# Long convolutions by a folded radix-8 DFT in an SSM and MLP kernel, forward and backward

## The chip, the cores and the metric

The kernel runs on one core of a Trainium2 chip. The metric is the device time of one execution in microseconds (us); lower is better. TensorE (PE) multiplies matrices, VectorE (DVE), ScalarE (ACT) and GpSimd (POOL) work on tiles of 128 partitions in SBUF, and the transfers (DMAs) of this program are issued by SyncE (SP) and, in the kernel before, by POOL too.

## The reference

A sequence of 2048 tokens with 512 channels runs twice through a layer normalisation, a gated long convolution and an MLP, with the same weights both times; the outputs are the result and the gradients of all inputs but B_x.

```python
def _A_ref(q, k, v, shift_k, ssm_k, ssm_D):
    for t in range(ks):                                  # ks = 4
        k_shift = k_shift + k_pad[:, t:t + S, :] * shift_k[:, ks - 1 - t][None, None, :]
    kv = k_shift * v
    L = 2 * S
    ...
    y_f = kv_f * kf_f[None, :, :, :]                     # rfft of length L of kv and of ssm_k, zero-padded
    y = irfft2(y_f, s=(1, L), ...).astype(jnp.bfloat16)[:, 0, :S, :]
    y = y + kv * ssm_D[None, None, :]
    return q * y

def _B_ref(x, w1, b1, w2, b2):
    h = _gelu(jnp.einsum("bsd,df->bsf", x, w1) + b1)     # F = 1376
    return jnp.einsum("bsf,fd->bsd", h, w2) + b2

x = A_q
x = x + _A_ref(_layernorm(x), A_k, A_v, A_shift_k, A_ssm_k, A_ssm_D)
x = x + _B_ref(_layernorm(x), B_w1, B_b1, B_w2, B_b2)
x = x + _A_ref(_layernorm(x), ...)
x = x + _B_ref(_layernorm(x), ...)
```

The convolution y depends on k, v and ssm_k alone, so it is computed once, and its result gates both layers. Backward, the gradient gy of y goes through the same convolution with a conjugated spectrum, which gives gkv (and from it the gradients of v, k and shift_k) and gh (of ssm_k).

## The kernel before, in words

The program has five parts, one after the other: the convolution forward (phase_conv_forward), the weights (load_weights), the MLP lanes forward and backward (phase_mlp: four slices of 512 tokens that run interleaved through both layers), the weight gradients (weight_grads), and the convolution backward (phase_conv_backward). A framework's scheduler sets the order of the instructions on each engine; an engine then takes its instructions strictly in that order, and SP issues its DMAs in that order too.

The long convolution is a real DFT of length 4096 written as dense matmuls. fwd_transform folds the 16 token tiles with their mirror images, tile a with tile 15-a, where the mirror is a matmul with an anti-identity into rev_ps and the sums P and differences M are made on DVE (L167, L168). Then it multiplies with cosine and sine tables for 8 blocks of even and 8 of odd frequencies: 8 matmuls into fwd_psc (L182) and 8 into fwd_pss (L185) for each of 16 pairs, 256 matmuls of 128x128 by 512 in all. It runs for h (ssm_k), for kv, and backward for gy. inv_transform does the same the other way in 264 matmuls (inv_A, L198 to L207); it runs for y, and backward for gkv and gh. The tables Fblk and Iblk have 8 MB each in bf16. gen_block_pair makes them: integer arguments on DVE and ACT (L132 to L137), sines on ACT (L138, L139). They are stored to DRAM (Fmat, Imat) and loaded again where they are used.

Around the transforms stand spec_products (six DVE instructions on 128x512 for each of 16 pieces of a spectrum, L228 to L240, the other operand streamed as sst from Hspec_d or KVspec_d), the shift convolution (four shifted loads kj of k for each tile, multiplied on DVE with Wbc, the shift weights broadcast to all partitions, L361 to L373), and backward process_gk, which shifts gks with matmuls (sh_ps), multiplies and adds on DVE (gk_tmp, gk_acc, L983 to L987), and gathers the shift weights' gradient with products on POOL (gw_prod, L994) and sums in f32 on DVE (gwacc, L995). WT_d (L303) is the shift weights transposed element by element in DRAM.

load_weights loads w1 and w2 and their transposes w1T and w2T from DRAM with DMA transposes; since 1376 is 10 x 128 + 96, the last 96 rows of w1T come as plain DMAs of 96x128 single elements (L543). The lanes read the tokens in natural order (x_sl, L827).

Of the kernel before, what the change touches and what calls it, by code (L numbers as in the profile page):

```python
# [11 lines left out]
ACT = mybir.ActivationFunctionType  # L12
# [36 lines left out]


def build_consts(nc, tc, const_pool, dims: Dims):
    c = Consts()
    S, L = dims.S, dims.L
    NJ = dims.NJ
    c.ident = const_pool.tile([P, P], BF16, name="ident")
    tmpf = const_pool.tile([P, P], F32, name="tmpf")
    nc.gpsimd.memset(tmpf, 0.0)
    nc.gpsimd.affine_select(out=tmpf, in_=tmpf, compare_op=ALU.not_equal, fill=1.0, base=0,
                            pattern=[[-1, P]], channel_multiplier=1)
    nc.vector.tensor_copy(out=c.ident, in_=tmpf)  # L60
    c.anti = const_pool.tile([P, P], BF16, name="anti")
    tmpf2 = const_pool.tile([P, P], F32, name="tmpf2")
    nc.gpsimd.memset(tmpf2, 0.0)
    nc.gpsimd.affine_select(out=tmpf2, in_=tmpf2, compare_op=ALU.not_equal, fill=1.0, base=-(P - 1),
                            pattern=[[1, P]], channel_multiplier=1)
    nc.vector.tensor_copy(out=c.anti, in_=tmpf2)
    alt_i = const_pool.tile([P, 4], I32, name="alt_i")
    nc.gpsimd.iota(alt_i[:, 0:1], pattern=[[0, 1]], base=0, channel_multiplier=1)
    altf = const_pool.tile([P, 4], F32, name="altf")
    nc.vector.tensor_copy(out=altf[:, 0:1], in_=alt_i[:, 0:1])  # L70
    nc.vector.tensor_single_scalar(out=alt_i[:, 1:2], in_=alt_i[:, 0:1], scalar=1, op=ALU.bitwise_and)
    nc.vector.tensor_copy(out=altf[:, 1:2], in_=alt_i[:, 1:2])
    nc.vector.tensor_scalar(out=altf[:, 2:3], in0=altf[:, 1:2], scalar1=-2.0, scalar2=1.0,
                            op0=ALU.mult, op1=ALU.add)
    c.altcol = const_pool.tile([P, 1], BF16, name="altcol")
    nc.vector.tensor_copy(out=c.altcol, in_=altf[:, 2:3])
    c.onescol = const_pool.tile([P, 1], BF16, name="onescol")
    nc.vector.memset(c.onescol, 1.0)
    c.onescol_f = const_pool.tile([P, 1], F32, name="onescol_f")
    nc.vector.memset(c.onescol_f, 1.0)  # L80
    hs_i = const_pool.tile([1, P], I32, name="hs_i")
    nc.gpsimd.iota(hs_i, pattern=[[1, P]], base=0, channel_multiplier=0)
    hs_f = const_pool.tile([1, P], F32, name="hs_f")
    nc.vector.tensor_single_scalar(out=hs_i, in_=hs_i, scalar=1, op=ALU.bitwise_and)
    nc.vector.tensor_copy(out=hs_f, in_=hs_i)
    nc.vector.tensor_scalar(out=hs_f, in0=hs_f, scalar1=-1.0, scalar2=0.5, op0=ALU.mult, op1=ALU.add)
    c.halfsign = const_pool.tile([1, P], BF16, name="halfsign")
    nc.vector.tensor_copy(out=c.halfsign, in_=hs_f)
    c.eps = const_pool.tile([P, 1], F32, name="eps")
    nc.vector.memset(c.eps, EPS_LN)  # L90
    c.SIN_EPS = 1e-6
    c.pibias = const_pool.tile([P, 1], F32, name="pibias")
    nc.vector.memset(c.pibias, math.pi * (1.0 - c.SIN_EPS))
    HT = dims.HT
    pv_i = const_pool.tile([P, 3 * HT], I32, name="pv_i")
    nc.gpsimd.iota(pv_i[:, 0:HT], pattern=[[2 * P, HT]], base=1, channel_multiplier=2)
    nc.gpsimd.iota(pv_i[:, HT:2 * HT], pattern=[[2 * P, HT]], base=0, channel_multiplier=2)
    nc.gpsimd.iota(pv_i[:, 2 * HT:3 * HT], pattern=[[2 * P, HT]], base=1, channel_multiplier=2)
    c.pv = const_pool.tile([P, 3 * HT], F32, name="pv")
    nc.vector.tensor_copy(out=c.pv, in_=pv_i)  # L100
    c.pvF = c.pv[:, 0:HT]
    c.pvIe = c.pv[:, HT:2 * HT]
    c.pvIo = c.pv[:, 2 * HT:3 * HT]
    ph_i = const_pool.tile([P, 2 * HT], I32, name="ph_i")
    nc.vector.tensor_single_scalar(out=ph_i, in_=pv_i[:, HT:3 * HT], scalar=L // 2, op=ALU.add)
    c.twc = const_pool.tile([P, 2 * HT], F32, name="twc")
    c.tws = const_pool.tile([P, 2 * HT], F32, name="tws")
    sin_scale = -(math.pi / L) * (1.0 - c.SIN_EPS)
    nc.scalar.activation(out=c.tws, in_=pv_i[:, HT:3 * HT], func=ACT.Sin, scale=sin_scale, bias=c.pibias)
    nc.scalar.activation(out=c.twc, in_=ph_i, func=ACT.Sin, scale=sin_scale, bias=c.pibias)  # L110
    c.ntwc = const_pool.tile([P, 2 * HT], F32, name="ntwc")
    nc.vector.tensor_single_scalar(out=c.ntwc, in_=c.twc, scalar=-1.0, op=ALU.mult)
    c.sin_scale = sin_scale
    return c


def build_row_tables(nc, pool, consts, dims):
    NJ = dims.NJ
    consts.row_e = pool.tile([P, NJ], F32, name="row_e")
    consts.row_o = pool.tile([P, NJ], F32, name="row_o")  # L120
    ri = pool.tile([P, NJ], I32, name="gen_ri")
    nc.gpsimd.iota(ri, pattern=[[2, NJ]], base=0, channel_multiplier=0)
    nc.vector.tensor_copy(out=consts.row_e, in_=ri)
    nc.gpsimd.iota(ri, pattern=[[2, NJ]], base=1, channel_multiplier=0)
    nc.vector.tensor_copy(out=consts.row_o, in_=ri)


def gen_block_pair(nc, tc, work_pool, consts: Consts, dims: Dims, row_tab, pv_col, out_cos, out_sin):
    NJ = dims.NJ
    L = dims.L  # L130
    u = work_pool.tile([P, NJ], I32, name="gen_u", tag="gen_u")
    nc.vector.tensor_scalar(out=u, in0=row_tab, scalar1=pv_col, scalar2=None, op0=ALU.mult)  # L132
    rs = work_pool.tile([P, NJ], I32, name="gen_rs", tag="gen_rs")
# [16 lines left out]
def gen_inverse_blocks(nc, tc, work_pool, consts, dims, dest_fn):  # L150
    for b in range(dims.HT):
# [3 lines left out]
                       dest_fn(Q_ICO, b), dest_fn(Q_ISO, b))  # L155


def fwd_transform(nc, tc, dims, consts, psum_pool, pm_pool, in_tiles, blocks, evac_pair, evac_nyq):
    D, HT, NT = dims.D, dims.HT, dims.NT
    Pt = []  # L160
    Mt = []
# [985 lines left out]
```

## Time and profile before

| | |
|---|---|
| median of 3 runs | 1572.46 us (1571.51 to 1572.75) |
| the profiled execution | 1560.17 us, its span 1558.4 us, mean granted TensorE clock 0.817 |
| busy | PE 989.9 us, DVE 920.9, ACT 503.9, POOL 259.5 |
| DMA | 213.44 MB in 329431 packets |

All rows of the prediction come from the one profiled execution. Its page lists busy time, the chain of work that ended last, and groups of instructions by line. In a windows row stand the stretch in us, its length, then for each engine its busy time and number of instructions, then the granted TensorE clock, the DMA share (the summed packet time against 16 DMA engines; it passes 1 where packets overlap) and GB/s. In a chain row stand start, length and what the path waited for. In a group's row stand line, engine, operation, output and inputs, shape, count, busy us, mean ns of one, and the idle time before it.

### The profile page before, as it was taken

To read this page: it belongs to the slowest core of one execution; us is meant where nothing else is said; L and a number is where in the kernel's file an instruction comes from. 1 tells how busy PE (TensorE), PEld (TensorE's weight loads), DVE (VectorE), ACT (ScalarE), POOL (GpSimd) and SP (SyncE) were. 2 spreads that over 40 slices of the span, in tenths; PEclk is the share of its full clock that TensorE was granted. 3 is DMA by queue.
4 is the path that set the end of the run, shared out by engine and by line. 5 is a ranking of instruction groups with operands and counts; after the bars stand their busy time and mean duration, and the time that the engine had idled before them with its cause. 6 is when DMAs were issued, how large, how long until landed. Compare 5 with 4: busy or idle time off the path is not lost.

```text
span 1558.4 us, 12837 instructions
## 1 busy us (share of the span) xinstructions
PE 989.9 (64%) x4028; PEld 403.3 (26%) x4109; DVE 920.9 (59%) x1840; ACT 503.9 (32%) x632; POOL 259.5 (17%) x369
## 2 busy tenths in 40 slices
PE   3557492095016688685998875999586276731097
PEld 2113141042002233232443332444132022200043
DVE  8669950721058999873788880000411699897921
ACT  7623471010007988892022230000022022221421
POOL 0036320020013111100001110000000055562000
PEclk9879696597557889997999987999688688865599
DMA  5557537407994464557785579898613421211201
GB/s 54 209 190 236 180 134 286 132 0 18 91 106 137 136 177 133 181 172 205 218 229 152 166 176 217 175 195 171 234 43 135 175 65 58 67 58 38 73 1 55
DMA packets 329431, 213.44 MB, mean 137 GB/s; under 512 B 213584, under 2 KB 322061, under 8 KB 328722
## 3 DMA queue, kind: packets, MB, share of 16 engines
q1 hardware_dynamic: 321474, 168.56, 46.3%
q0 software_dynamic: 7888, 44.05, 7.4%
q8 instruction: 32, 0.52, 0.1%
q14 instruction: 37, 0.30, 0.1%
HBM read 91.27 MB, written 85.67 MB: 114 GB/s over the span
## 4 chain that ended last, share of the span: by engine, by line
DVE 31%; PE 30%; DMA 15%; SPq 9%; issue 6%; ACT 5%; POOL 3%; another core or an unknown queue 1%; DVEq 0%; POOLq 0%; ACTq 0%
PE dw_ps L784 9%; PE fwd_psc L182 4%; PE fwd_pss L185 4%; DVE gwacc L995 3%; DVE gk_tmp L986 3%; DMA kj<-in_A_k_dram 2%; PE inv_A L198 2%; DMA KVspec_d<-KVspec 2%; SPq L541 2%; PE inv_A L200 2%; SPq L306 2%; PE gh_ps L694 2%; DMA sst<-Hspec_d 2%; PE inv_A L204 2%; PE inv_A L206 2%
## 5 line engine op out<-in xcount | busy, mean ns | idle before, releaser
L675 PE MATMUL o_ps<-w_sb,h_sl 128*128 128x512 bf16 x347 | 97.2, 422 | 32.6 <-DVE h_sl L644 32.1
L897 DVE TENSOR_TENSOR gd_prod<-gy_bf,kv_t 128x512 bf16<-128x512 bf16 x16 | 6.4, 424 | 172.8 <-PE gd_ps L898 166.1
L662 PE MATMUL z_ps<-nT_sl,w_sb 128*128 128x512 bf16 x342 | 83.1, 394 | 20.7 <-DMA nT_sl<-n_sl 14.4
L694 PE MATMUL gh_ps<-gT_sl,w2T_sb 128*128 128x512 bf16 x343 | 82.8, 387 | 20.5 <-DMA gT_sl<-G 19.5
L784 PEld LDWEIGHTS <-dw_tm 128*128 128x128 bf16 x704 | 69.1, 98 | 102.6 <-DMA dw_tm<-h_d 18.0
L784 PE MATMUL dw_ps<-G,dw_tm 128*128 128x512 bf16 x345 | 77.9, 386 | 17.9 <-DMA dw_tm<-h_d 17.5
L705 PE MATMUL gn_ps<-w1T_sb,gz_sl 128*128 128x512 bf16 x346 | 82.1, 383 | 0.2
L696 DVE SCALAR_TENSOR_TENSOR gz_sl<-gh_ps,gpb 128x512 bf16<-128x512 f32 x88 | 58.3, 688 | 30.5 <-PE gh_ps L694 26.6
L784 PE MATMUL dw_ps<-dw_n,dw_tm 128*128 128x512 bf16 x345 | 75.8, 379 | 0.4
L672 PE MATMUL o_ps<-x_sl,ident 128*128 128x512 bf16 x32 | 13.5, 421 | 89.7 <-DVE x_sl L621 87.4
L750 ACT ACTIVATE nb_sl<-nb_sl,ab_ab 128x512 bf16<-128x512 bf16 x32 | 23.4, 802 | 145.1 <-DVE bb_junk L708 125.6
L994 POOL TENSOR_TENSOR gw_prod<-sh_bf,k_t 128x512 bf16<-128x512 bf16 x48 | 58.9, 1229 | 43.5 <-DVE gwacc L995 32.5
L198 PE MATMUL inv_A<-KVspec,Iblk 128*128 128x512 bf16 x63 | 25.3, 401 | 64.2 <-DVE KVspec L262 64.0
L787 ACT ACTIVATE dw_o<-dw_ps 128x512 bf16<-128x512 f32 x22 | 13.1, 597 | 154.9 <-PE dw_ps L784 148.6
L995 DVE TENSOR_TENSOR gwacc<-gwacc,gw_prod 128x512 f32<-128x512 f32 x64 | 60.8, 962 | 1.4 <-POOL gw_prod L994 1.4
L664 ACT ACTIVATE g_z<-z_ps,b1col 128x512 bf16<-128x512 f32 x88 | 54.5, 692 | 20.8 <-PE z_ps L662 13.2
L198 PE MATMUL inv_A<-GYspec,Iblk_b 128*128 128x512 bf16 x63 | 25.2, 400 | 49.4 <-DVE GYspec L262 49.1
L182 PE MATMUL fwd_psc<-P,Fblk 128*128 128x512 bf16 x124 | 40.2, 452 | 25.6 <-ACT h_b L336 16.3
L675 PEld LDWEIGHTS <-h_sl 128*128 128x128 bf16 x352 | 34.3, 105 | 84.0 <-DVE h_sl L644 37.7
L598 ACT ACTIVATE n_sl<-x_sl,ln_nmr,rstd 128x512 bf16<-128x512 bf16 x32 | 24.7, 819 | 94.0 <-POOL ln_nmr L591 94.0
L953 POOL MEMSET shm_f<- 128x128 f32 x3 | 0.6, 205 | 314.7 <-DVE P1spec L240 314.1
L662 PEld LDWEIGHTS <-w_sb 128*128 128x128 bf16 x352 | 34.8, 100 | 67.1 <-issue 25.4
(273 smaller groups left out, 2358.5 us busy)
## 6 DMA issues: line engine op xcount, KB each, us to landing
sst<-Hspec_d SPq DMA_DIRECT2D x64, 128.0 KB, 2.1
n_d<-n_sl SPq DMA_DIRECT2D x16, 512.0 KB, 3.7
h_d<-h_sl SPq DMA_DIRECT2D x16, 512.0 KB, 2.8
gp_d<-g_p SPq DMA_DIRECT2D x16, 512.0 KB, 3.0
nb_sl<-n_d SPq DMA_DIRECT2D x16, 512.0 KB, 4.4
gpb<-gp_d SPq DMA_DIRECT2D x16, 512.0 KB, 5.2
gz_d<-gz_sl SPq DMA_DIRECT2D x16, 512.0 KB, 3.5
kj<-in_A_k_dram SPq DMA_DIRECT2D x61, 128.0 KB, 2.8
```

The lines of the kernel that those rows point to most:

```text
L182: nc.tensor.matmul(psc, lhsT=blocks(qc, a)[:, b * P:(b + 1) * P], rhs=inc[a], start=(a == 0), stop=(a == HT - 1))
L185: nc.tensor.matmul(pss, lhsT=blocks(qs, a)[:, b * P:(b + 1) * P], rhs=ins[a], start=(a == 0), stop=(a == HT - 1))
L198: nc.tensor.matmul(A1, lhsT=blocks(Q_ICE, b)[:, cols], rhs=spec[:, 0, b, :], start=first, stop=False)
L662: nc.tensor.matmul(ps, lhsT=w.w1[:, dc, c * P:(c + 1) * P], rhs=nT[:, dc, :], start=(dc == 0), stop=(dc == ND - 1))
L664: nc.scalar.activation(out=zb[:, c - c0, :], in_=ps, func=ACT.Identity, bias=w.b1col[:, c:c + 1])
L675: nc.tensor.matmul(ps, lhsT=h[:, c, t * P:(t + 1) * P], rhs=w.w2[:, c, :], start=False, stop=(c == NFC - 1))
L694: nc.tensor.matmul(ps, lhsT=w.w2T[:, dc, c * P:(c + 1) * P], rhs=gT[:, dc, :], start=(dc == 0), stop=(dc == ND - 1))
L696: nc.vector.scalar_tensor_tensor(out=gz[:, c, :], in0=ps, scalar=1.0, in1=gp[:, c - c0, :], op0=ALU.mult, op1=ALU.mult, accum_out=m.b1part ...
L705: nc.tensor.matmul(ps, lhsT=gz[:, c, t * P:(t + 1) * P], rhs=w.w1T[:, c, :], start=(c == 0), stop=(c == NFC - 1))
L784: nc.tensor.matmul(ps, lhsT=tm[:, i, t, :], rhs=rhs, start=(i == 0 and t == 0), stop=(i == 1 and t == NT - 1))
L994: nc.gpsimd.tensor_tensor(out=prod, in0=sh[jj], in1=kt, op=ALU.mult)
L995: nc.vector.tensor_tensor(out=gwacc[:, jj, :], in0=gwacc[:, jj, :], in1=prod, op=ALU.add)
```

## The change

What it does, part by part:

- **Tokens.** The sequence is cut in 4 blocks of 512. Of each block, tile positions 0 and 1 hold tokens 0 to 255 and positions 2 and 3 hold tokens 511 down to 256, so that a token and its mirror image stand on one partition. This order is kept through kv, y, the MLP lanes and gy. Mirrored halves come from DRAM copies in reversed row order (vB, hB, qB, goB, kB) that flip_rows makes by one DRAM to DRAM DMA each, and results that are stored mirrored (o0B, o1B, o3B) are put back by unflip_rows. tok_io loads or stores a block as two DMAs.
- **Transforms.** Fold makes the sums and differences of a signal with its mirror and across the 4 blocks by a few large DVE instructions (X, S, D), and streams() those of one of five groups of frequencies, k = k1 + 8j for k1 = 0, 4, 2, 1, 3. fwd_group needs 112 matmuls over all groups (145 for h, with the ends of the blocks and ssm_D worked in as extra rows sp5), inv_group 112, and gh 228 of width 257. inv_blocks turns the eight slots of W into the four blocks on DVE. product is the spectrum product in five large DVE instructions for each of 8 pieces.
- **Tables.** tabF and tabN have 2 MB each; sin_of makes them with the argument on POOL, a mask on DVE and the sine on ACT, in pieces of 128x1024. The inverse tables are DMA transposes of them.
- **Shift convolution.** k is transposed on PE into kT; ks and backward gk are matmuls with diagonal weight matrices wdiag (256 of 128x128 by 128 each); gw is a matmul of gks with shifted loads kj, summed in PSUM, and read by its diagonal.
- **Weights.** w1T and w2T are 15 DMA transposes from the loaded w1 and w2 in SBUF.

```diff
+def flip_rows(nc, out, src2d, first, n=256):
+    rs = src2d.ap[0][0]
+    nc.sync.dma_start(out=out, in_=bass.AP(tensor=src2d.tensor, offset=src2d.offset + first * rs,
+                                           ap=[[512 * rs, out.shape[0]], [-rs, n], [1, src2d.shape[1]]]))
...
+def tok_io(nc, sb, ap2d, flipped, i, store=False):
+    lo = ap2d[i * 512:i * 512 + 256, :].rearrange("(t p) d -> p t d", p=P)
+    hi = flipped[i].rearrange("(t p) d -> p t d", p=P)
...
+class Fold:
+    def __init__(self, nc, pool, lo, hi, integer):
...
+        tt(out=X[:, 0], in0=lo, in1=hi, op=ALU.add)
+        tt(out=X[:, 1], in0=lo, in1=hi, op=ALU.subtract)
...
+        tt(out=self.S, in0=X[:, :, 0:2], in1=X[:, :, 2:4], op=ALU.add)
+        tt(out=self.D, in0=X[:, :, 0:2], in1=X[:, :, 2:4], op=ALU.subtract)
...
+def product(nc, pool, A, B, Rb, g, out, conj):
...
+        tt(out=t, in0=A[:, :, s], in1=B[:, :, s], op=ALU.mult)
+        tt(out=out[:, 0, s], in0=t[:, 0], in1=t[:, 1], op=op_r)
...
+            tt(out=u[:, 0], in0=A[:, 1, s], in1=B[:, 0, s], op=ALU.mult)
+        tt(out=u[:, 1], in0=A[:, 0, s], in1=B[:, 1, s], op=ALU.mult)
+        tt(out=out[:, 1, s], in0=u[:, 0], in1=u[:, 1], op=op_z)
...
+def inv_blocks(nc, pool, W, N, last=False):
...
+    tt(out=PN, in0=W[:, :, 4:6], in1=W[:, :, 6:8], op=ALU.add)
+    tt(out=MW, in0=W[:, :, 4:6], in1=W[:, :, 6:8], op=ALU.subtract)
+    tt(out=G[:, :, 0], in0=W[:, :, 0], in1=W[:, :, 1], op=ALU.add)
+    tt(out=G[:, :, 1], in0=W[:, :, 0], in1=W[:, :, 1], op=ALU.subtract)
+    tt(out=B0, in0=G, in1=W[:, :, 2:4], op=ALU.add)
+    tt(out=B1, in0=G, in1=W[:, :, 2:4], op=ALU.subtract)
...
+    flip_rows(nc, dram.hB[1:4], dram.hT, 512)
...
+            tok_io(nc, ksb, out3, dram.o3B, i, store=True)
+            for h in range(4):
+                kj = io.tile([P, 4, D], BF16, name="kj", tag="kj", bufs=2)
...
+                    nc.tensor.matmul(gw[cc], lhsT=gks[:, 4 * i + h, cs], rhs=kj[:, :, cs],
+                                     start=(i == 0 and h == 0), stop=(i == 3 and h == 3))
...
+        unflip_rows(nc, out3, dram.o3B)
...
+    for c in range(NFC):
+        nc.sync.dma_start_transpose(out=w.w2T[:, :, c * P:(c + 1) * P], in_=w.w2[:, c, :])
     for dc in range(ND):
-        rows = w1_ap[dc * P:(dc + 1) * P, :]
-        nc.sync.dma_start_transpose(out=w.w1T[:, 0:nfull, dc * P:(dc + 1) * P], in_=rows[:, 0:nfull * P])
-        if nfull < NFC:
-            nc.sync.dma_start_transpose(out=w.w1T[0:F - nfull * P, nfull, dc * P:(dc + 1) * P],
-                                        in_=rows[:, nfull * P:F])
...
+        nc.sync.dma_start_transpose(out=w.w1T[:, :, dc * P:(dc + 1) * P], in_=w.w1[:, dc, :])
...
-                nc.sync.dma_start(out=x, in_=tok(q_ap, s))
+                tok_io(nc, x, q_ap, dram.qB, s)
```

How the order of instructions moves is shown at three places. The first is the start of SP's queue. Before, a row gives line, operation, output and input and the shape that the DMA writes; hn is ssm_k, Dbc and Wbc are the broadcast D and shift weights.

```order
L298 DMA hn<-in_A_ssm_k_dram 128x4x2048
L303 DMA WT_d<-in_A_shift_k_dram 2048x1x1
L306 DMA Dbc_158<-in_A_ssm_D_dram 128x512
L305 DMA Wbc_157<-WT_d 128x512 x4
L363 DMA kj<-in_A_k_dram 128x512
L361 DMA kj<-in_A_k_dram 127x512
```

In the changed kernel the same engine issues, from its eighth DMA on (vB's flip is its first), with hT the transposed ssm_k, kn tiles of k, hsp the extra rows and Hspec_d, ks_d stored results:

```order
L360 DMA hT_d<-hT 128x16x512
L389 DMA wdiag_d<-wdiag 128x2048
L396 DMA kn<-in_A_k_dram 128x4x512
L147 DMA hB_d<-hT_d 768x1x512
L363 DMA hB_d<-hT_d 2x256x256
L368 DMA hsp<-hT_d 4x512
L396 DMA kn<-in_A_k_dram 128x4x512
L366 DMA hB<-hB_d 128x8x512
```

The flip of hB now stands behind the store of wdiag, which needs DVE, and the load of hB behind both flips. Further down the same queue of the changed kernel, around the spectrum of h:

```order
L147 DMA qB_d<-in_A_q_dram 1024x1x512
L427 DMA ks_d<-ksb 128x2048
L164 DMA vt<-in_A_v_dram 128x2x512
L164 DMA vt<-vB_d 128x2x512
L427 DMA ks_d<-ksb 128x2048
L445 DMA Hspec_d<-Hg 256x1x1024 x2
L147 DMA goB_d<-in_grad_out_dram 1024x1x512
L445 DMA Hspec_d<-Hg 256x1x2048 x2
L147 DMA kB_d<-in_A_k_dram 1036x1x512
L445 DMA Hspec_d<-Hg 256x1x2048
L481 DMA_TRANSPOSE tabI<-tabF_d 128x16x128 x4
L460 DMA Hg_997<-Hspec_d 128x2x1024
```

Three flips that the convolution does not need (q, grad_out, k) now stand ahead of the inverse table and the first loaded piece of the spectrum, Hg_997. The second place is the weights on SP. Before:

```order
L541 DMA_TRANSPOSE w1T_sb<-in_B_w_dram 128x10x128
L543 DMA w1T_sb<-in_B_w_dram 96x128x1
L541 DMA_TRANSPOSE w1T_sb<-in_B_w_dram 128x10x128
L543 DMA w1T_sb<-in_B_w_dram 96x128x1
L527 DMA w_sb<-in_B_w_dram 128x4x1376
L529 DMA w_sb<-in_B_w_dram 128x10x512
L538 DMA w_sb<-in_B_w_dram 96x512
L541 DMA_TRANSPOSE w1T_sb<-in_B_w_dram 128x10x128
```

In the changed kernel:

```order
L675 DMA w_sb<-in_B_w_dram 128x4x1376
L677 DMA w_sb<-in_B_w_dram 128x10x512
L684 DMA w_sb<-in_B_w_dram 96x512
L688 DMA_TRANSPOSE w1T_sb<-w_sb 128x11x128
L686 DMA_TRANSPOSE w2T_sb<-w_sb 128x4x128 x11
L688 DMA_TRANSPOSE w1T_sb<-w_sb 128x11x128 x3
```

The single-element DMAs are gone, and the transposes follow the loads. The third place is the convolution backward, where gks (the gradient of the shifted k) is shifted, multiplied and summed. On DVE before:

```order
L983 TENSOR_TENSOR gk_acc<-gks_t,Wbc_b 128x512 x2
L995 TENSOR_TENSOR gwacc<-gwacc,gw_prod 128x512
L986 TENSOR_TENSOR gk_tmp<-sh_bf,Wbc_b 128x512 x2
L987 TENSOR_TENSOR gk_acc<-gk_acc,gk_tmp 128x512
L995 TENSOR_TENSOR gwacc<-gwacc,gw_prod 128x512
L987 TENSOR_TENSOR gk_acc<-gk_acc,gk_tmp 128x512
```

On DVE in the changed kernel there (vb is v, ksb_b the shifted k, gkv the gradient of kv):

```order
L539 TENSOR_TENSOR gks<-gkv,vb 128x2048
L540 TENSOR_TENSOR ksb_b<-gkv,ksb_b 128x2048
L539 TENSOR_TENSOR gks<-gkv,vb 128x2048
L540 TENSOR_TENSOR ksb_b<-gkv,ksb_b 128x2048
L572 TENSOR_TENSOR gwm<-gw_6439,ident 128x128 x4
L572 TENSOR_TENSOR gwm<-gw_6440,ident 128x128
L573 TENSOR_REDUCE gwo<-gwm 128x4
```

And on SP in the changed kernel at the end of that stretch:

```order
L162 DMA out_dram<-ksb_b 128x2x512
L162 DMA o3B_d<-ksb_b 128x2x512
L551 DMA kj<-in_A_k_dram 128x512 x2
L554 DMA kj<-kB_d 128x512 x4
L153 DMA out_dram<-o3B_d 4x256x512
L554 DMA kj<-kB_d 128x512 x4
L585 DMA out_dram<-gk_o 128x512 x3
L612 DMA KVb<-KVspec_d 128x2x2048
```

The shifts and sums have left DVE; in their place stand shifted loads, the last four of them behind the unflip of out_3.

More of the change, by code (lines that the diff above doesn't have):

```diff
@@ L840, in phase_mlp @@
         m.G = [G3, G1]
[L841 removed]
+        for i in range(NSL):
+            tok_io(nc, G3[:, i * TS:(i + 1) * TS, :], go_ap, dram.goB, i)
         with tc.tile_pool(name="m_gb", bufs=2, reuse_waits="tile") as m.gpool:
```

1103 lines of the change are left out of this document (507 added, 596 removed).

## The prediction

> **What bounds the kernel now.** I read the page's head first, then the span cut into stretches, then the chain of waits inside those where no engine is full, and last the groups for prices.
>
> The head of the page shows that no engine is busy throughout.
>
> ```profile
> span 1558.4 us, 12837 instructions
> PE 989.9 (64%) x4028; PEld 403.3 (26%) x4109; DVE 920.9 (59%) x1840; ACT 503.9 (32%) x632; POOL 259.5 (17%) x369
> ```
>
> So shares say little; the stretches carry the argument. Columns: stretch, length, busy us of PE, weight load, DVE, ACT, POOL with counts, granted clock, DMA share, GB/s.
>
> ```profile
> 0.00:90.00 90.00, 37.71 (x142) 14.86 (x145) 60.67 (x124) 55.54 (x56) 6.45 (x20) 0.85 0.59 153
> 90.00:200.00 110.00, 70.86 (x255) 26.80 (x260) 101.86 (x177) 47.12 (x57) 57.29 (x79) 0.80 0.58 190
> 200.00:245.00 45.00, 44.00 (x201) 19.89 (x203) 17.22 (x27) 29.15 (x40) 8.20 (x15) 1.00 0.27 98
> 245.00:293.00 48.00, 0.00 (x0) 0.00 (x0) 17.38 (x53) 0.00 (x0) 0.59 (x2) 0.53 0.79 306
> 293.00:372.00 79.00, 61.90 (x266) 26.36 (x272) 33.53 (x80) 8.96 (x15) 18.47 (x17) 0.88 0.07 21
> 372.00:447.00 75.00, 0.36 (x1) 0.06 (x1) 11.55 (x38) 0.60 (x1) 0.00 (x0) 0.51 1.57 75
> 447.00:712.00 265.00, 194.18 (x753) 75.46 (x768) 229.41 (x346) 214.10 (x228) 40.66 (x64) 0.87 0.50 155
> 712.00:928.00 216.00, 177.70 (x764) 75.01 (x781) 162.40 (x455) 42.94 (x60) 25.63 (x64) 0.92 0.72 195
> 928.00:964.00 36.00, 18.43 (x86) 8.17 (x86) 3.88 (x5) 3.70 (x6) 0.00 (x0) 0.82 0.97 193
> 964.00:1097.00 133.00, 132.33 (x596) 59.77 (x608) 0.00 (x0) 10.75 (x18) 0.00 (x0) 0.99 0.85 178
> 1097.00:1136.00 39.00, 15.37 (x33) 2.82 (x32) 16.21 (x31) 0.60 (x1) 0.00 (x0) 0.60 0.66 255
> 1136.00:1196.00 60.00, 58.05 (x251) 25.64 (x256) 5.80 (x15) 19.11 (x32) 0.00 (x0) 0.95 0.08 27
> 1196.00:1245.00 49.00, 11.05 (x32) 3.55 (x34) 29.41 (x90) 0.00 (x0) 2.34 (x10) 0.61 0.59 225
> 1245.00:1440.00 195.00, 103.36 (x334) 36.44 (x339) 177.44 (x288) 39.84 (x70) 99.04 (x99) 0.72 0.19 57
> 1440.00:1500.00 60.00, 17.29 (x74) 7.31 (x77) 45.20 (x108) 19.70 (x30) 0.00 (x0) 0.61 0.18 49
> 1500.00:1558.00 58.00, 47.32 (x249) 21.16 (x252) 8.89 (x14) 11.79 (x20) 0.78 (x1) 0.94 0.09 37
> ```
>
> The reader sees five parts: convolution forward to 372, weights to 447 (PE idle), MLP lanes and weight gradients to 1097, which the change leaves alone but for their loads and stores, and convolution backward from 1097 on, 461 us, of which 195 are DVE at 177 busy (shifts and sums of gks). PE-full stretches of the transforms are 200:245, 1136:1196, 1500:1558 and most of 293:372.
>
> **Prices.** Rows of the chain, with start, length and what was waited for:
>
> ```profile
> 2.16 31.67 SPq L306
> 33.83 17.65 another core or an unknown queue
> 53.77 10.18 DMA kj<-in_A_k_dram
> 372.40 13.57 SPq L541
> 423.86 15.62 SPq L547
> 443.20 1.44 SPq L547
> 1112.34 23.49 DMA Fblk_b<-Fmat
> 1136.08 3.57 PE fwd_psc L182 x8
> 1142.59 1.73 PE fwd_psc L182 x8
> ```
>
> Eight matmuls of width 512 take 1.73 us at full clock (0.216 each), 3.57 after an idle stretch. A DMA transpose holds SP 1.44 us. Weight loads take 98 ns each (59.77 us for 608 in 964:1097). The weights' stretch is waits of 13 to 16 us on SP beside the single-element DMAs.
>
> Groups (line, engine, operation, shapes, count, busy us, mean ns) and transfers (KB each, us to landing):
>
> ```profile
> L228 DVE TENSOR_TENSOR pr_t<-KVspec,sst 128x512 bf16<-128x512 bf16 x16 | 6.8, 423 | 19.3 <-PE fwd_pss L185 19.3
> L644 DVE TENSOR_TENSOR h_sl<-g_s,g_z 128x2048 bf16<-128x2048 bf16 x16 | 19.5, 1218 | 4.6 <-ACT g_s L640 4.5
> L995 DVE TENSOR_TENSOR gwacc<-gwacc,gw_prod 128x512 f32<-128x512 f32 x64 | 60.8, 962 | 1.4 <-POOL gw_prod L994 1.4
> L711 POOL TENSOR_SCALAR bb_diag<-ident,bb_cols 128x128 bf16<-128x128 bf16 x32 | 16.6, 518 | 169.0 <-DVE bb_junk L708 168.2
> L591 POOL TENSOR_SCALAR ln_nmr<-ln_nmr 128x4 f32<-128x4 f32 x16 | 5.1, 320 | 1.4
> L122 POOL IOTA gen_ri<- 128x1024 int32 x1 | 1.0, 971 | 0.0
> kj<-in_A_k_dram SPq DMA_DIRECT2D x61, 128.0 KB, 2.8
> KVspec_d<-KVspec POOLq DMA_DIRECT2D x1, 4096.0 KB, 33.0
> kv_d<-kvt POOLq DMA_DIRECT2D x1, 2048.0 KB, 8.7
> dw_n<-n_d SPq DMA_DIRECT2D x2, 2048.0 KB, 17.5
> dw_tm<-h_d SPq DMA_TRANSPOSE x22, 4.6
> ```
>
> A bf16 DVE instruction goes from 423 ns at 512 elements to 1218 at 2048, 0.52 ns an element; so I estimate 0.69 us at 1024 and 2.28 at 4096.
>
> **The flips** are what no row shows: 1 MB, DRAM to DRAM, 1024 rows of 1 KB in reversed order, source with an outer dimension of 4. The nearest rows: WT_d, also DRAM to DRAM with an outer 4, was issued at the start and gone by 51.5 (the first two chain rows): about 49 us for 2048 elements. While it ran nearly alone, this row has a DMA share of 0.20 at 4 GB/s, that is some 3 to 4 of 16 engines:
>
> ```profile
> 33.00:51.00 18.00, 12.47 (x35) 3.10 (x35) 17.90 (x30) 17.81 (x18) 0.00 (x0) 1.00 0.20 4
> ```
>
> The first kj of the chain has 127 rows instead of 128 and took 10.18 us instead of 2.8: about 8 us over a fixed 2 for 127 KB-rows, 64 ns each, as if on one engine. On four engines a flip is 256 rows each: 16 + 2 = 18 us at 64 ns, 26 us at WT_d's 96 ns (49 / 512). On all sixteen it would be half of kv_d's 8.7, 4.4 us; on one, 1024 x 64 ns = 66 us. I take 20, nearer to kj's rows, which are as long. The two pieces of hB have outer sizes of 3 and 2, which no row shows; I take 38 for both together.
>
> The Trainium skill (DMA: Bandwidth & Descriptors, "Why a DMA increments its semaphore by 16 and not by 1") says that the number of engines is the largest one up to 16 that divides the slowest dimension of both sides. It speaks against this change: by it 4 engines serve a flip, and 3 and 2 engines serve hB's pieces, 256 descriptors each, which gives the same 38; with four engines throughout hB would cost about 10 us less and the sum be 1188. The trace agrees for 127 rows (10.18 us against 2.8).
>
> **The sum, part by part.**
>
> *Convolution forward, 372 to 248.* Removed: 24 MB of table stores and loads, the store of KVspec with its 33.0 us (245:293), half of the matmuls. New path: POOL makes the sine arguments, 16 pieces of 128x1024 and 10 small ones. The trace has no such piece: below, IOTA at 0.97; above, from 320 ns at 4 and 518 at 128 elements, 1.6 ns each, 1.95 us. I take 1.95, as it is the same operation: 31 + 5 + 6 for the start = 42. The diagonal weights stand on DVE behind the last mask, and SP's queue behind their store, so hB's flips start at about 50: 50 + 38 + 5 for the load = 93. Fold of h: two instructions at 1024 by two halves and two at 4096, with the first streams 13: 106. PE 145 x 0.216 = 31, with a cold start 35: 141. Meanwhile vB's flip is hidden beside POOL, but those of q, grad_out and k follow hB's load on SP, 3 x 20 from about 100: 160, and the inverse table's transposes (4, overlapped, 8 us) and the spectrum's load (4) stand behind them: first product at 172. This, not PE, is the later one. Then DVE: eight products of 1.22 + 4 x 0.69 = 4.0 make 32, streams of kv 8, the last inverse on PE and ACT 9, inv_blocks with y twice 13.5: 248. The sines on ACT and the shift matmuls (256 small ones) lie beside POOL and the flips; without that cover the matmuls would cost 256 x 0.098 = 25 us. Ends: 215 and 280.
>
> *Weights, 75 to 30.* 15 transposes x 1.44 = 22, the last x load and the waits around 8. w1 and w2 load beside inv_blocks. Ends: 20 and 42.
>
> *Lanes and weight gradients, 650 to 673.* The same instructions on PE, DVE and ACT. The unflip of out_0 stands before the loads that start the backward lanes: 20, less 5 of cover. That of out_1 stands between weight-gradient transposes with three buffers ahead (each 32 matmuls, 7 us): 8 remain. The doubled loads and stores lie beside PE. Ends: +0 and +45.
>
> *Convolution backward, 461 to 247.* From its start: tabF 2 MB between 8.7 and 17.5, 14. gy's 112 matmuls 26, cold start included: 40. Products begin with the first group, DVE 32 + 8 in all, last inverse 9, inv_blocks 27: 82 (gd and the 24 us table load of 8 MB are gone). First shifted loads with 127 rows, 10; then 16 rounds of four kj at about 2.4 (4 issues, two buffers) 38: 130. The POOL products and DVE sums that filled 195 us are gone, and these loads are late next. The unflip of out_3 before the last four kj: 150. 256 small matmuls for gk at 0.098, 25: 175. Table transposes behind 16 stores: 10. 228 matmuls of width 257, at weight-load pace 22, and 4 to the last evacuation: 211. inv_blocks for four channel pieces, 14 instructions of half size, 8.3 each: 244, last store 3. Ends: 215 and 290.
>
> By the Trainium skill (VectorE: DVE Perf Modes, "Mode 2×_1P — pack two bf16 into one 32-bit read") packing needs unit steps from a 4-byte boundary, which slices that start at element 1 do not have; were all of these instructions to run unpacked, I estimate 1.9 times 33, and 1228 in sum. No row has width 257.
>
> 1558 - 124 - 45 + 23 - 214 = 1198. The profiled run lies 2 us above its span, and the median 12 above that run; a shorter run should show less of either, and with the doubtful terms rather taken dear I say 1198 for the median. That is 24% below now, far above the 0.2% that a measurement of this kernel can tell.
>
> **Rivals.**
>
> 1. *Flips are cheap*, spread over all engines (4.4 us). For it: 2 MB moved in 8.7. Against it: WT_d's share of 0.20. hB 93 becomes 65, the h spectrum ends at 113 and the first product starts at about 130 instead of 172, and out_0, out_1, out_3 give back 15, 8 and 16: 1198 - 42 - 39 = 1117. Chance 0.17.
> 2. *Everything on SP's queue dearer*: flips at 26 (seven on the path, +42), POOL at 2.8 us (+14), DVE unpacked at the end (+15): 1269. For it: the 962 ns that DVE needs at 512 unpacked elements (L995, with POOL beside it). Chance 0.2.
> 3. *Slower than now*: a negative step keeps each flip on one engine, 66 us. Eight on the path x 46 = 368 brings the sum to 1566, and hB's second piece to about 1590. It decides from about 45 us more per flip. For it: kj with 127 rows on one engine; against it: WT_d's share. Chance 0.04.
> 4. *PE's halved work hides behind DVE and transfers*, so that it gives nothing: it is in the sum, since I counted DVE's and SP's chain, not matmuls.
>
> The forecast, 1150 to 1240, has 0.58; the little left is for mishaps on either side. Below 1105 and above 1285 lie about 2 in 10 together. Only rival 3 is slower (0.04), and only it passes close to no change (0.01): faster 0.95.
>
> **What would show it.** Each flip's landing near 18 to 26 us, with later DMAs of SP behind it; h's first matmul at about 106 and the first product at 172; PE idle before both; the lanes starting at about 280 with no 13 us waits before them; backward about 247 long, with DVE idle in the kj rounds. Wrong it goes if flips land in 5 or in 60 us, if POOL's pieces differ by half, or if DVE's large instructions on strided halves do not hold 0.52 ns an element.

## The result and the profile after

The changed kernel takes 1254.38 us (median of 4 runs, 1253.47 to 1255.86) against 1571.99 for the kernel before: ratio 0.7983, 95% interval 0.797 to 0.7997. I had said 1198, with a range of 1105 to 1285: the direction and the range hold, the change is 56 us smaller than forecast, and the time lies above the narrower 1150 to 1240 to which I gave a chance of 0.58. The profiled run's span is 1252.4 us.

The head of the page after the change:

```profile
span 1252.4 us, 10780 instructions
PE 789.9 (63%) x3765; PEld 353.5 (28%) x3765; DVE 672.1 (54%) x1316; ACT 433.3 (35%) x538; POOL 97.5 (8%) x173
```

PE lost 200 us of work, DVE 249, POOL 162; their shares of the span fell too, and only ACT's rose, from 32 to 35%. The stretches of the changed kernel, cut at its own events (first spectrum product, y done, first load of x, last stores of the forward lanes, last lane matmul, first and last weight-gradient matmul, gkv done, last kj round, first and last matmul of gh), with the same columns as in the prediction:

```profile
0.00:159.00 159.00, 68.56 (x473) 36.09 (x473) 58.34 (x120) 59.88 (x77) 30.63 (x43) 0.83 0.61 180
159.00:254.00 95.00, 57.81 (x216) 22.32 (x216) 60.13 (x84) 30.96 (x36) 0.00 (x0) 0.79 0.27 97
254.00:280.00 26.00, 0.00 (x0) 0.00 (x0) 0.63 (x6) 0.00 (x0) 0.11 (x1) 0.50 0.78 160
280.00:548.00 268.00, 192.43 (x768) 74.64 (x768) 238.80 (x378) 211.81 (x225) 40.54 (x64) 0.87 0.51 152
548.00:758.00 210.00, 169.87 (x735) 71.10 (x735) 151.06 (x427) 42.49 (x60) 23.92 (x60) 0.93 0.70 187
758.00:805.00 47.00, 9.44 (x34) 3.14 (x33) 13.46 (x30) 4.38 (x7) 1.97 (x4) 0.61 0.74 125
805.00:967.00 162.00, 156.05 (x704) 69.64 (x704) 0.00 (x0) 12.54 (x21) 0.00 (x0) 0.97 0.84 170
967.00:1073.00 106.00, 54.59 (x226) 22.36 (x224) 75.45 (x102) 33.55 (x39) 0.00 (x0) 0.78 0.33 97
1073.00:1152.00 79.00, 39.17 (x207) 19.13 (x208) 15.83 (x21) 11.06 (x21) 0.00 (x0) 0.61 0.67 206
1152.00:1180.00 28.00, 12.74 (x178) 11.72 (x176) 12.88 (x62) 6.77 (x13) 0.35 (x1) 0.80 0.69 209
1180.00:1213.00 33.00, 29.15 (x228) 23.35 (x228) 23.21 (x40) 19.18 (x42) 0.00 (x0) 0.85 0.14 30
1213.00:1252.00 39.00, 0.09 (x1) 0.00 (x0) 22.31 (x54) 0.67 (x2) 0.00 (x0) 0.56 0.14 54
```

Against the prediction's four terms: convolution forward 254 us (I said 248, before 372), weights 26 (30, before 75), lanes and weight gradients 687, from 280 to 967 (673, before 650), convolution backward 285 (247, before 461). The convolution forward and the weights came out within 6 us of the forecast, and 52 of the missing 54 us of span lie behind them: 14 in the lanes and weight gradients, 38 in the backward convolution.

Four places in the trace of the changed kernel show work waiting. First SP's queue in the convolution forward (start, length on the queue, line, output and input):

```profile
45.85 0.89 SPq L147 DMA_DIRECT2D hB_d<-hT_d  x1
46.78 9.02 SPq L363 DMA_DIRECT2D hB_d<-hT_d  x1
67.11 0.36 SPq L366 DMA_DIRECT2D hB<-hB_d  x1
116.47 11.64 SPq L445 DMA_DIRECT2D Hspec_d<-Hg  x2
128.16 0.66 SPq L147 DMA_DIRECT2D kB_d<-in_A_k_dram  x1
139.04 15.49 SPq L481 DMA_TRANSPOSE tabI<-tabF_d  x4
154.63 0.58 SPq L460 DMA_DIRECT2D Hg<-Hspec_d  x1
```

The load of hB is issued 21 us after its first flip; both pieces together took what I had taken for one. The transposes and the first spectrum load follow k's flip, as foreseen. Second, DVE's timeline; the brackets give how long it sat idle before the instruction, and what ended that:

```profile
159.19 0.29 DVE L257 COPY spec_rb<-Hg 128x512 bf16<-128x512 bf16 x1 [19.78 <-DMA Hg<-Hspec_d]
180.84 1.22 DVE L242 TENSOR_TENSOR pr_t<-KVg,Hg 128x2048 bf16<-128x2048 bf16 x1 [7.15 <-ACT KVg L231]
201.24 1.23 DVE L242 TENSOR_TENSOR pr_t<-KVg,Hg 128x2048 bf16<-128x2048 bf16 x1 [9.00 <-ACT KVg L231]
219.69 1.23 DVE L242 TENSOR_TENSOR pr_t<-KVg,Hg 128x2048 bf16<-128x2048 bf16 x1 [11.03 <-ACT KVg L231]
1028.67 0.69 DVE L243 TENSOR_TENSOR Yb<-pr_t 128x1024 bf16<-128x1024 bf16 x1 [21.60 <-PE iv_ps L281]
```

DVE waits in three of the groups of the forward convolution for the spectrum of kv, and in the backward convolution 21.6 us for PE. Third, SP where the lanes end:

```profile
774.58 0.47 SPq L162 DMA_DIRECT2D o1B_d<-nb_sl  x1
775.10 15.59 SPq L906 DMA_DIRECT2D dw_n<-n_d  x2
790.73 24.34 SPq L920 DMA_TRANSPOSE dw_tm<-h_d  x6
```

In the kernel before, five of the transposes dw_tm were issued from 908.56 on, ahead of the lanes' last store at 921.57 and of dw_n at 937.22; now dw_n comes first, and PE stands from 758 to 805 with 9 us of work. Fourth, the end (what SP waited for, in all, times, longest):

```profile
SPq L1071 <- DMA out_dram<-gdo: 11.5, 1, 11.5
```

### The profile page after: what moved, and what is told of

Same layout as the page of the kernel before. It is cut to its first block, busy times and chain, and to the rows that moved or that the text cites. A ratio compares the mean times of both kernels' runs of the same rounds, so it can differ in the third digit from the quotient of the medians.

```text
span 1252.4 us, 10780 instructions
## 1 busy us (share of the span) xinstructions
PE 789.9 (63%) x3765; PEld 353.5 (28%) x3765; DVE 672.1 (54%) x1316; ACT 433.3 (35%) x538; POOL 97.5 (8%) x173
## 5 line engine op out<-in xcount | busy, mean ns | idle before, releaser
L835 PEld LDWEIGHTS <-w2T_sb 128*128 128x128 bf16 x352 | 35.4, 101 | 64.7 <-DMA gT_sl<-G 15.3
L557 PE MATMUL gw<-kj,gks 128*128 128x512 bf16 x64 | 26.5, 561 | 32.9 <-DMA kj<-kB_d 20.6
L846 PEld LDWEIGHTS <-gz_sl 128*128 128x128 bf16 x352 | 34.7, 99 | 40.6 <-issue 2.0
L781 ACT ACTIVATE g_s<-g_t 128x2048 bf16<-128x2048 bf16 (+1 forms) x24 | 42.5, 1772 | 9.3 <-DVE g_t L780 9.3
L778 ACT ACTIVATE g_q<-g_z 128x2048 bf16<-128x2048 bf16 (+1 forms) x24 | 42.9, 1787 | 0.1
L278 PE MATMUL iv_ps<-Yg,tabI 128*128 128x512 bf16 x56 | 19.5, 453 | 36.7 <-DVE Yg L243 33.2
```

The source lines that it names most:

```text
L557: nc.tensor.matmul(gw[cc], lhsT=gks[:, 4 * i + h, cs], rhs=kj[:, :, cs], start=(i == 0 and h == 0), stop=(i == 3 and h == 3))
L778: nc.scalar.activation(out=q, in_=zb, func=ACT.Square)
L781: nc.scalar.activation(out=sg, in_=t, func=ACT.Sigmoid)
L835: nc.tensor.matmul(ps, lhsT=w.w2T[:, dc, c * P:(c + 1) * P], rhs=gT[:, dc, :], start=(dc == 0), stop=(dc == ND - 1))
L846: nc.tensor.matmul(ps, lhsT=gz[:, c, t * P:(t + 1) * P], rhs=w.w1T[:, c, :], start=(c == 0), stop=(c == NFC - 1))
```

## The experiments

My theory A: the forecast's missing part is the order on SP's queue (dw_n, tabIb, the element-wise store of out_6) and the alternation of DVE and PE by groups, and a flip (a copy of rows in reversed order) costs what it does because few DMA engines serve it. The rivals: these waits are covered, so that taking one away changes little; and a flip's rows cost the same on however many engines. Differences are stated in us on a kernel of 1248: (ratio - 0.7985) x 1563, with 0.7985 from the changed kernel's second measurement (below). Intervals of about 0.002 to 0.003 on each ratio make 3 to 5 us.

**Flips as unreversed copies with an outer dimension of 256 rows.**

```diff
-    nc.sync.dma_start(out=out, in_=bass.AP(..., offset=src2d.offset + first * rs,
-                                           ap=[[512 * rs, out.shape[0]], [-rs, n], [1, src2d.shape[1]]]))
+    nc.sync.dma_start(out=out.rearrange("i q c -> q i c"),
+                      in_=bass.AP(..., offset=src2d.offset + (first - n + 1) * rs,
+                                  ap=[[rs, n], [512 * rs, out.shape[0]], [1, src2d.shape[1]]]))
```

> Every flip becomes a copy of the same rows in unreversed order whose outer dimension is 256 rows instead of 4 blocks (the reversal is left out, since a DMA with a negative step in its outer dimension does not compile; bytes, row length and place in the queue stay). Theory A (a flip is slow because four DMA engines serve it, and SP's queue passes that on): the load of hB is issued some 13 us sooner than at 67, the first spectrum product comes at about 145 instead of 160, the lanes and the end of the kj rounds gain 5 to 8 each, in all 25 to 35 us: about 1222. Rival B (the row copies themselves cost, or the flips are covered by the sines and by PE): less than 10 us, 1245 or more.

Ratio 0.7648 (0.763 to 0.7666): 53 us less, more than theory A said. Two things go beyond what I wrote ahead: the second piece of hB is here 256 rows of 1 KB, where it was 512 of 512 B, and k's copy has 272 rows of a block instead of 259. On SP (this run) wdiag's store and hB's flips and load:

```profile
22.57 0.36 SPq L389 DMA_DIRECT2D wdiag_d<-wdiag  x1
32.92 0.59 SPq L146 DMA_DIRECT2D hB_d<-hT_d  x1
42.81 0.37 SPq L366 DMA_DIRECT2D hB<-hB_d  x1
242.34 0.39 SPq L165 DMA_DIRECT2D x_sl<-in_A_q_dram  x1
```

The two pieces take 10 us instead of 21. The share of the DMA engines that are busy (the column before the last; GB/s behind it) says why. In the changed kernel, first while hB's piece of 3 blocks is moved, then that of 2 blocks, then, alone, the flip of k with 4:

```profile
50.00:59.00 9.00, 5.78 (x98) 5.36 (x95) 0.64 (x6) 4.43 (x8) 0.00 (x0) 1.00 0.20 72
61.00:64.00 3.00, 0.00 (x0) 0.00 (x0) 0.00 (x0) 0.00 (x0) 0.00 (x0) 0.50 0.14 44
133.00:139.00 6.00, 5.80 (x23) 1.78 (x21) 2.01 (x4) 3.09 (x4) 0.00 (x0) 1.00 0.27 97
```

and in this run, while the copies of q, grad_out and k are moved beside stores of h's spectrum, and after them:

```profile
68.00:82.00 14.00, 11.55 (x44) 3.41 (x44) 3.86 (x7) 5.51 (x6) 0.00 (x0) 0.97 1.03 332
84.00:86.00 2.00, 2.00 (x6) 0.51 (x5) 0.00 (x0) 0.00 (x0) 0.00 (x0) 0.50 0.01 2
```

Of 16 engines 0.20 is three, 0.14 two and 0.27 four. At 72 and 44 GB/s the 768 and 256 KB of hB take 11 and 6 us: the two pieces were moved one after the other. By the rule of the Trainium skill that the prediction named (DMA: Bandwidth & Descriptors, "Why a DMA increments its semaphore by 16 and not by 1") it is three and two engines as well, and four for a whole flip, and the trace agrees. The three unreversed copies, 3.2 MB, were done within 16 us of the first one's issue at 67.5; at the 97 GB/s of four engines they would have taken 33. Each busy engine moves 20 to 22 GB/s in all these rows, so neither the reversal nor the number of blocks changes much of what one engine moves. Further, the first spectrum product comes at 112 (theory A: 145), and the first x load comes at 242.3, against 274.5 in the second run of the changed kernel. Some of these 32 us are order: wdiag's store, for which hB's flips had waited on SP, is issued at 22.6 here instead of 45.0, and the first flip 13 us earlier. The weight gradients gain 9 (153 us from first to last matmul instead of 162); I put that down to out_1's unflip, which no longer holds their transposes.

**The inverse table ahead of the spectrum tiles.**

```diff
-        tabI = wp.tile([P, 2, 16, 256], BF16, name="tabIb")
-        load_inverse_table(nc, tabI, dram.tabF)
...
+    tabI = tip.tile([P, 2, 16, 256], BF16, name="tabIb")
...
         nc.sync.dma_start(out=tabF, in_=dram.tabF)
+        load_inverse_table(nc, tabI, dram.tabF)
```

> The inverse table tabIb of the backward convolution is loaded before the spectrum tiles Hb, not after them. Theory A (DVE's 21.6 us of idling at 1007 to 1028 is the table's four transposes, which SP could not issue while it waited to reuse a tile Hb): the gap shrinks to a few us, about 1235. Rival B (PE's transform of gy would be the next wait): under 8 us, 1247 or more.

Ratio 0.7928 (0.79 to 0.7956): 9 us less. DVE's gap:

```profile
1015.86 0.69 DVE L243 TENSOR_TENSOR Yb<-pr_t 128x1024 bf16<-128x1024 bf16 x1 [8.53 <-PE iv_ps L281]
```

The gap went from 21.6 to 8.5, and gkv was ready 13 us sooner, so the table was the cause of 13 of the 21.6; 8.5 us of waiting for PE stay. The scheduler issued the table's transposes from 765 on, between the lanes and the weight gradients, and that gap is 3 us longer here. The result lies between the two expectations, nearer to the rival's.

**dw_n after the first dw_tm.**

```diff
-        for i, l in ((0, 3), (1, 1)):
-            nc.sync.dma_start(out=nres[:, i, :, :], in_=m.n_d[l].rearrange("(t p) d -> p t d", p=P))
...
+                if which == 0 and c == 5:
+                    for i, l in ((0, 3), (1, 1)):
+                        nc.sync.dma_start(out=nres[:, i, :, :], in_=m.n_d[l].rearrange("(t p) d -> p t d", p=P))
```

> The two 2 MB loads dw_n are issued after the first transposes dw_tm of the weight gradients, instead of before them. Theory A (PE's 55 us without work between the lanes and the weight gradients, 18 before the change, comes from dw_n standing ahead of dw_tm on SP): the weight gradients start some 20 us sooner, of which about 10 may come back as a later wait for dw_n; 1234 to 1244. Rival B (the gap is the late last store of the lanes, and dw_tm waits for that anyway): under 5 us.

Ratio 0.7927 (0.7906 to 0.7947): 9 us less. The first group of weight-gradient matmuls (first and last start), in this run and then in the second run of the changed kernel:

```profile
L926 PE MATMUL dw_ps<-G,dw_tm x352: 379/379/634, 786.3 to 877.2; 128*128 128x512 bf16 x176
```

```profile
L925 PE MATMUL dw_ps<-G,dw_tm x345: 379/379/634, 800.8 to 886.9; 128*128 128x512 bf16 x173
```

They start 14.5 us sooner and take 5 longer, while dw_n is now moved beside the transposes that follow. Theory A holds, with the give-back that it named. The gap itself, from the last lane matmul to the first of these, was 47 us in the changed kernel and 10 before, not the 55 and 18 that I wrote ahead. Some 30 us of it stay: the transposes still stand behind the lanes' last store.

**out_6 in rows.**

```diff
-            nc.sync.dma_start(out=out6.rearrange("(c p) -> p c", p=P), in_=gdo)
+        nc.tensor.matmul(ps[0:ND, 0, 0:P], lhsT=gdo, rhs=consts.ident, start=True, stop=True)
+        gdr = hp.tile([ND, P], BF16, name="gdr")
+        nc.vector.tensor_copy(out=gdr, in_=ps[0:ND, 0, 0:P])
+        nc.sync.dma_start(out=out6.rearrange("(c p) -> c p", p=P), in_=gdr)
```

> out_6 is turned on PE to 4 rows of 128 and stored in rows, instead of 512 single elements. Theory A (the last 12 us after DVE's last instruction are that store): 1254 falls by 8 to 10 us, to about 1245. Rival B (they are the last stores of gh, or the end of the program): under 3 us.

Ratio 0.7902 (0.7885 to 0.7918): 13 us less, a little more than expected. The kernel's last transfer, 1 KB as 512 single elements, cost 13 us that nothing hides.

**The changed kernel again.**

> The changed kernel once more, unaltered, so that it stands on the chip of the next three. Both theories: ratio 0.798 to the kernel before, as measured first.

Ratio 0.7985 (0.797 to 0.7999); 1248.33 us beside 1563.4 for the kernel before on that chip. The stretches agree with the first profile, but for a convolution forward that is 5 us shorter.

**Flips on POOL's queue.**

```diff
-    nc.sync.dma_start(out=out, in_=bass.AP(tensor=src2d.tensor, ...
+    nc.gpsimd.dma_start(out=out, in_=bass.AP(tensor=src2d.tensor, ...
```

> All flips and unflips are issued by POOL on its own queue instead of SP; same access patterns, so the same few engines serve them. Theory A1 (what a flip costs is mostly that later DMAs of SP's queue stand behind it): 30 to 45 us less than the changed kernel, near what spreading the rows gave (52 us). Theory A2 (the cost is the few engines themselves, for whoever needs the flipped rows or those engines): under 15 us.

Ratio 0.7947 (0.7922 to 0.7972): 6 us less, so A2: the few engines are the cost, more than the place in SP's queue. This run also shows how long a flip takes from issue to landing (KB, then us):

```profile
qB_d<-in_A_q_dram POOLq DMA_DIRECT2D x1, 1024.0 KB, 14.6
out_dram<-o1B_d POOLq DMA_DIRECT2D x1, 1024.0 KB, 19.1
```

The seven whole flips and unflips land in 14.6 to 21.4 us. hB's load still follows its first flip by 21 us (38.3 to 59.7 on the two queues). The first product comes 11 us sooner, but its inverse then waits for tabI, which SP issues at 142 to 156 as late as before, and y is ready only 3 us sooner. The unflip of out_1, no longer held behind the dw_tm transposes, ran beside them, and the weight gradients began 10 us later.

**Flips as two DMAs of two blocks.**

```diff
+    for a, b in [(0, 2), (2, 4)]:
+        nc.sync.dma_start(out=out[a:b], in_=bass.AP(..., ap=[[512 * rs, b - a], [-rs, n], [1, src2d.shape[1]]]))
```

> Each flip of four blocks becomes two DMAs of two blocks each (rows, bytes and reversal as before; hB's two pieces are left). Theory A (the outer dimension sets the number of engines): two engines with 512 rows each, so a flip lasts about 35 us instead of 18, and the kernel is 20 to 50 us slower. Rival B (price per row over all, not per engine): within 8 us.

Ratio 0.8177 (0.816 to 0.8193): 30 us more. Same rows, same bytes, half the outer dimension. While v's two pieces are moved at the start of this run:

```profile
6.00:19.00 13.00, 0.00 (x0) 0.00 (x0) 5.03 (x8) 8.03 (x7) 10.96 (x8) 1.00 0.14 48
```

Two engines move 48 GB/s where four moved 97, and the second piece does not run beside the first. With 256 as outer dimension 53 us less (order in it), with 2 instead of 4 30 more: the outer dimension sets the price, and rival B falls.

**The new load_weights in the kernel before.** The edit is the diff of load_weights as shown, alone.

> The kernel before with load_weights alone taken from the changed kernel. The prediction's term (transposes from SBUF instead of single-element DMAs, 75 us down to 30): 40 to 48 us less than before, about 0.972. Rival (the w1 and w2 loads, which the transposes now wait for, take the place of the removed wait, since nothing runs beside them here): 25 us or less.

Ratio 0.9809 (0.9789 to 0.9829): 30 us less, between the two. First and last start of the first MLP matmuls, in the kernel before and in this one:

```profile
L662 PE MATMUL z_ps<-nT_sl,w_sb x342: 376/379/634, 473.6 to 693.2; 128*128 128x512 bf16 x171
```

```profile
L655 PE MATMUL z_ps<-nT_sl,w_sb x346: 376/379/635, 415.3 to 662.5; 128*128 128x512 bf16 x173
```

They start 58 us sooner and end 31 sooner: the scheduler now loads two slices of x ahead of the weights and the other two only at 421, and the lanes, which interleave less, give 27 back. In the changed kernel all x loads follow the weights and the lanes take their full 218 us; the stretch is 26 us there. The wait was removed as I had it, and what a removed wait brings depended on what the order then did.

**The flips of grad_out and k in the forward lanes.**

```diff
-    flip_rows(nc, dram.goB, aps["grad_out"].flatten_outer_dims(), 511)
-    flip_rows(nc, dram.kB, aps["A_k"].flatten_outer_dims(), 511, n=259)
...
+                    if s == 1:
...
+                        nc.sync.dma_start(out=t[0, 0:1, :], in_=x[0:1, 0, :])
+                        flip_rows(nc, t, src, 511, n=n)
```

> The flips of grad_out and k are moved from the convolution forward into the forward lanes (each stands there behind a one-row store of x, which makes it wait), with four engines as before. Theory A (in the convolution forward these two hold the inverse table and the spectrum's first load): the first spectrum product comes at about 140 instead of 154, and 8 to 12 us are won there; the lanes, whose transposes now stand behind the flips, give back up to that: 1238 to 1250. Rival B (PE's transform of kv and the groups' alternation end at the same time anyway): the convolution forward itself stays within 3 us.

Ratio 0.8037 (0.8004 to 0.8071): 8 us slower. First load of x and first backward load in this run:

```profile
262.73 0.39 SPq L162 DMA_DIRECT2D x_sl<-in_A_q_dram  x1
557.19 0.38 SPq L162 DMA_DIRECT2D G<-in_grad_out_dram  x1
```

The convolution forward gains the 12 us of theory A (262.7 instead of 274.5), and the lanes lose 22 (294.5 between the two loads instead of 272.7). I had allowed the lanes to give back 12, so the total misses theory A's range. The two flips cost about 11 us each where they now stand, as long as four engines need for 1 MB at 97 GB/s.

**The groups overlapped.**

```diff
+    kvg(0)
     for g, (k1, base, n) in enumerate(GROUPS):
...
-        fwd_group(nc, psum, tabF, fk.streams(k1), g, KV)
+        KV = KVs[g]
+        if g + 1 < len(GROUPS):
+            kvg(g + 1)
```

> In the convolution forward the transform of group g+1 of kv is written ahead of the product and the inverse of group g. Theory A (from the first product at 154 to y at 248 are 94 us where I summed 76, because DVE waits 7 to 11 us in each group for the next group's spectrum, which PE makes only after the inverse of the last): 8 to 15 us less, 1233 to 1240. Rival B (PE is busy or cold through this stretch, so that order doesn't matter): under 3 us.

Ratio 0.7864 (0.7838 to 0.789): 19 us less, above theory A's range. The longest of DVE's waits for KVg is now

```profile
171.32 1.22 DVE L242 TENSOR_TENSOR pr_t<-KVg,Hg 128x2048 bf16<-128x2048 bf16 x1 [4.10 <-ACT KVg L231]
```

and the first load of x stands at 256.3. In my sum DVE's 40 us of products and streams followed each other without a break; in the kernel they did not.

**All of it together.**

> All four changes of order together (tabIb early, dw_n after the first dw_tm, the two flips in the lanes, groups overlapped) and out_6 stored in rows. If each wait stands alone, the gains add: 9 + 9 + 13 and what the other two give, some 40 us, 1208. If they cover each other (rival): 1220 or more.

Ratio 0.7736 (0.7712 to 0.7761), 1209.34 us: 39 less. The single results sum to 9 + 9 + 13 + 19 - 8 = 42, so within the intervals these waits stand alone.

**The flips taken back out of the lanes, and issued by POOL in the forward part.** The edit is that of the last, without the flips in the lanes, and with gpsimd in flip_rows.

> As the four together, but grad_out's and k's flips stay in the convolution forward, and all flips there are issued by POOL; the three unflips stay on SP. The flips in the lanes cost 22 us there (x loads to the first backward load 294.5 us instead of 272.7) and won 12, so that leaving them out should give about 10 of 1209 back: 1199; POOL's queue gives 0 to 8 more by the earlier first product: 1190 to 1199. Rival (the flips on POOL's queue collide with the loads of the transform of kv, since the same engines serve both): 1200 or more.

Ratio 0.7635 (0.7618 to 0.7652), 1193.83 us: 55 less than the changed kernel, and the fastest kernel here with the full result.

## Why the prediction was right, and where it was off

*Convolution forward: 254 for 248, by two errors that cancel.* The order of the path was as written (flips, load of hB, fold, h, flips of q, grad_out and k, inverse table, products), but its terms were not. POOL's pieces took less than the 1.95 us I extrapolated,

```profile
8.82 1.42 POOL L138 TENSOR_SCALAR tab_u<-krow,pvn 128x1024 int32<-128x1024 f32 x1 [0.29 <-ACT tabN L141]
```

and hB's two flips took 21 us together instead of 38, since the rows were cheaper than I priced them (below). Against that, the three flips of q, grad_out and k did not follow one another: SP stood 11.6 us at the store of h's spectrum before it issued k's, a wait for ACT, which writes that spectrum, that I had taken for covered, and the transposes of the table held SP for 15.5 us instead of 8. The first product came at 159 instead of 172, partly by luck. From there to y I summed 76 and the trace has 95. The step that failed is "eight products ... make 32, streams of kv 8, the last inverse 9": a sum of DVE's instructions, where PE's transform and inverse of each group stood between them. The overlapped groups show 19 us for it.

*Weights: 26 for 30.* The row that priced a transpose held (11 in 14.28 us). Alone, in the kernel before, the same edit brings 30 and not 45.

*Lanes and weight gradients: 687 for 673.* Up to their last matmul the lanes took 479 us, where the kernel before took 469 and my sum had 15 more. The weight gradients themselves were shorter than before. In the kernel before, the gap ahead of them and they themselves:

```profile
916.00:925.50 9.50, 8.51 (x32) 2.90 (x31) 9.50 (x24) 0.74 (x2) 0.63 (x2) 0.78 1.08 235
925.50:1097.00 171.50, 153.20 (x691) 69.13 (x704) 5.81 (x9) 15.47 (x25) 1.35 (x3) 0.95 0.88 183
```

So the weight gradients went from 172 to 162 where I had added 8, and the gap from 10 to 47. The step that failed is that this gap was not in the sum at all, though the order of instructions showed dw_n ahead of dw_tm. The experiment with dw_n put off starts them 14.5 us sooner and gets 9 us back; what holds the rest is open.

*Convolution backward: 285 for 247.* Three terms. gkv was ready after 106 us, not 82. The 82 was too small by its own terms: products, streams, inverse and inv_blocks are 32 + 8 + 9 + 27 = 76, and they could not start before tabF had come at 14, so that 90 had to stand there. Of the rest 13 are by tabIb; its transposes stand behind the spectrum tiles Hb, for three of which SP stood 13.8 us until DVE had released earlier ones. The kj rounds took 79 where I had 68 with the unflip. And "last store 3" was 17, 11.5 of it waiting for out_6's single elements; stored in rows, it makes the kernel 13 us shorter. DVE's prices held nearly to the hundredth: 0.69 at 1024, 1.2 at 2048, 2.29 at 4096.

*The flips' price* was right in its mechanism, few engines by the outer dimension: spread over 256 rows the kernel is 53 us faster, in pieces of two blocks 30 slower. It was too dear in size. I took 64 ns for a row of 1 KB and as much for one of 512 B; four engines at 97 GB/s are 42 ns, and two at 44 GB/s are 23 ns for the short rows. So a flip is moved in 11 us and not 16, and hB's pieces in 11 and 6. On POOL's queue the landings, 14.6 to 21.4 us beside other transfers, lie around the 20 that I took. Rival 1 (cheap flips, 1117) did not occur, and the unreversed copies, with their change of order, show that it would have been worth some 53 us and not the 81 that I gave it. Rival 3 (one engine) is excluded by the same runs. Of rival 2, the flips were not dearer and POOL was cheaper.

*Unpacked DVE instructions at the end* did not occur. By the Trainium skill (VectorE: DVE Perf Modes, "Mode 2×_1P — pack two bf16 into one 32-bit read") a slice that starts at element 1 should not pack. Another page of the Trainium skill (Vector Engine (DVE) Microarchitecture Reference, "5.1 Performance modes — why throughput varies by op and dtype") says that 4-byte alignment makes no difference. The trace agrees with the second; these are one instruction on slices of width 257 that start at element 0, and one on slices that start at element 1, written backwards:

```profile
1212.98 0.69 DVE L644 TENSOR_TENSOR gh<-Wh 128x1028 bf16<-128x1028 bf16 x1
1213.58 0.69 DVE L647 TENSOR_TENSOR gh<-Wh 128x1020 bf16<-128x1020 bf16 x1
```

Both take 0.69 us, as 1024 elements do elsewhere. So the 22 us of the last stretch are the 33 of my sum, less what was already done beside gh's matmuls.

*Still open* is why the scheduler put dw_n first, and the some 30 us that stay between the lanes and the weight gradients; a version that issues dw_tm before the lanes' last store was not tried. No run here has a reversal that is spread over all engines.

## What to carry to other kernels

Price a DMA by its outer dimension before its bytes: a copy of 1 MB as 4 blocks of rows was moved at 97 GB/s here, by 4 of 16 engines, and whatever waits for it waits that long, on either queue; POOL's queue won 6 us, and moving two flips into the lanes lost 8. When a rewrite shortens the engines' work, sum the chain through every engine that a step passes, not the busiest engine's instructions, and read the new order on the queue that issues the loads: three of four missing terms stood there in plain sight (dw_n, the inverse table, the last store). Look at the last transfer of a program by itself; nothing hides it.

## What the runs showed of the hardware that I had not expected

Copies from DRAM to DRAM with 4, 3 and 2 outer blocks kept 0.27, 0.20 and 0.14 of the DMA engines busy and moved 97, 72 and 44 to 48 GB/s, 20 to 22 for each busy engine; two of them issued one after the other from SP's queue, with 3 and 2 blocks, were moved one after the other, 21 us from the first issue to the load behind them. 512 two-byte elements stored to DRAM held the program's end for 11.5 us; the same 512 as four rows of 128 left no such wait and made the kernel 13 us shorter. A DVE instruction on bf16 slices off the 4-byte boundary, with a reversed output, ran at the packed rate.
